# A second fp16 form of the exponential on VectorE, in a fused attention and feed-forward kernel

## The chip, the cores and the metric

One core of a Trainium2 chip runs the whole kernel. The metric is the device time of one execution in microseconds (us); lower is better. Engines are named as in the profile: PE (TensorE), DVE (VectorE), ACT (ScalarE), POOL (GpSimd), SP (SyncE, which issues the DMAs).

## What is computed

One transformer block in bf16 with S = 2048 tokens, width D = 512, 32 heads of 16, and a feed-forward part (FFN) of width 1792:

```python
def reference(A_x, A_wqkv, A_wo, B_x, B_w_gate, B_w_up, B_w_down):
    def _A_ref(x, wqkv, wo):
        ...
        scores = jnp.einsum("bhqd,bhkd->bhqk", q, k) * (Dh ** -0.5)
        p = _softmax(scores, axis=-1)
        o = jnp.einsum("bhqk,bhkd->bhqd", p, v)
        return (lambda x, *d: x.transpose(*d))(o, 0, 2, 1, 3).reshape(B, S, D) @ wo
    def _B_ref(x, w_gate, w_up, w_down):
        return (_gelu(x @ w_gate) * (x @ w_up)) @ w_down
    x = A_x
    h = x + _A_ref(_layernorm(x, axis=-1), A_wqkv, A_wo)
    h2 = h + _B_ref(_layernorm(h, axis=-1), B_w_gate, B_w_up, B_w_down)
    return h2
```

The softmax has 32 x 2048 x 2048 exponentials. They are most of the elementwise work.

## The kernel before

The program holds two complete versions of the block, one behind the other.

**`fast_path`** comes first. It does not subtract a row maximum. Queries are taken in chunks of 512, 512, 512, 256 and 256 rows (`CHUNKS`); a unit is one chunk times one group of four heads, so there are NU = 40 units, 24 of 512 rows and 16 of 256. The scores come transposed, in tiles of 128 keys x 512 columns, one PSUM bank each, 2048 tiles in all. `qk` multiplies the tiles, alternately three and two banks at a time (`SLOTS`), `exps` has ACT write exp of them to the bf16 ring `PT` (line 1221), and `pv` multiplies the result by `VA`, the values with a 17th column that sums the weights, into one accumulator bank. A share of the tiles goes to DVE instead: `dget` opens groups of up to four tiles, `dconv` (line 1527) converts a tile of scores to uint16 in `dX`, `dchain` (lines 1540 to 1547) makes two factors from the group by bit operations and multiplications, `dE2` and `dX`, and `pv` multiplies both by `VA` and adds them. Python code that runs before the launch lays out the order of all engines' instructions: a list of streams with priorities, estimated durations and gates (`Sched`). Groups are opened where that plan has DVE free: at most one in `DGAP` = 6 us, at most `NX` = 3 not yet consumed, and only when the chain of the group before has passed the point where `gw` counts up.

At a unit's end `ofin` copies the accumulator, transposes it and takes the reciprocal of the sums into `LINV`, a tile of 128 x 40 units x 16 columns (line 1621): 16 columns for a unit of 512 rows, `4 * nb` = 8 for one of 256. `consts` sets all of `LINV` to 1.0 at the start (line 1250). `masks` writes one column, `probe`, that shows how a float beyond uint16 is converted.

**The check and the guard.** Near the end `check` (from line 1782) compares: `LCHK` is `LINV` clipped from below and above, made 1.0 where the clipped value equals `LINV` and 0.0 where not, over all 640 columns, with the probe's comparison in column 641. The minimum of the row goes to `lmin`, a matmul sums the 128 partitions, and the sum is put in `flag`. Every engine ends its part of the fast path with this (line 1088 is the load of the flag):

```python
r = h.alloc_register("flag_" + name)
h.reg_load(r, flag[0:1, 0:1])
with h.If_ne(r, 128):
    for sem, v in fin:
        if v:
            h.wait_ge(sem, v)
    FP.run(name, h)
```

**`max_path`**, which `FP.run` issues, computes the same block from the inputs again, with the row maximum. Its units are 4 chunks x 8 head groups = 32 units of 64 tiles. A fixed order of ticks is written out: 32 ticks for a unit, and the second pass starts `P2_START` = 42 ticks behind the first. In a tick, PE multiplies two score tiles for the first pass (`p1_pair`, three banks in turn) and two for the second (`p2_pair`, three other banks in turn), as one group that has all waits in front; DVE takes the maximum of the first two (`p1_consume`, `tensor_reduce`, 128 x 512 from PSUM); ACT takes exp of the other two, one bank each (`p2_consume`). Every fourth tick eight products with the values follow (`pv_burst`), in the other ticks a piece of the dense work (projections, output product, FFN), whose results ACT evacuates. Per unit four small DMAs put the negated maximum into rows of `QT`. After the last tick the last chunk's output product and FFN run by themselves.

Of the kernel before, what the change touches and what calls it, by code (L numbers as in the profile page):

```python
# [163 lines left out]
BF16 = mybir.dt.bfloat16  # L164
# [889 lines left out]
GS = 4  # L1054
# [5 lines left out]
DGAP = 6.0  # L1060
DBUSY = 2.0
LN2 = 0.6931471805599453
CENTER = 40
EC, EB, EK = 0.45805388, 1.01669147, 0.16656247
VSCALE = 2.0 ** (127 - CENTER)


def bass_sequential_preLN__mha_block__geglu_ffn__prompt_kernel(nc, A_x, A_wqkv, A_wo, B_x, B_w_gate, B_w_up, B_w_down, out):
# [37 lines left out]
def fast_path(nc, P, base0, ARENA, pbank, flag, A_x, A_wqkv, A_wo, B_x, B_w_gate, B_w_up, B_w_down, out):  # L1106
# [3 lines left out]
    def at(name, shape, dt, off=None):  # L1110
        nb = DTS[dt]
        for d_ in shape[1:]:
            nb *= d_
        if off is None:
            off = cur[0]
            cur[0] = (off + nb + 31) // 32 * 32
        assert off + nb <= ARENA, ("SBUF arena overflow", name, off, nb, ARENA)
        return nc.alloc_sbuf_tensor_at(name, shape, dt, offset=base0 + off)
# [6 lines left out]
    offX = cur[0]  # L1125
    dX = at("dX", [128, NX, GS, 512], U16)
    dW = at("dW", [128, GS, 512], F16)
    dE2 = at("dE2", [128, NE, GS, 512], BF16)
    gset = at("gset", [128, 1], FP32)
    probe = at("probe", [128, 2], U16)  # L1130
    offE = cur[0]
# [88 lines left out]
    def ACTF(o, i, func, **kw):  # L1220
        return lambda e: e.activation(out=o, in_=i, func=func, **kw)  # L1221
# [23 lines left out]
    def consts():  # L1245
        yield Op("pool", 0.5, lambda e: e.memset(ones_bf[:], 1.0), writes=["ones_bf"])
        yield Op("pool", 0.3, lambda e: e.affine_select(out=ident[:], in_=ones_bf[:, 0:128], pattern=[[1, 128]], compare_op=ALU.is_equal, fill=0.0,
                                                        base=0, channel_multiplier=-1), reads=["ones_bf"], writes=["ident"])
        yield Op("pool", 0.1, lambda e: e.memset(nhalf[:], -0.5), writes=["nhalf"])
        yield Op("pool", 0.2, lambda e: e.memset(LINV[:], 1.0), writes=[("LINV", u) for u in range(NU)])  # L1250
        yield Op("pool", 0.1, lambda e: e.memset(zero_bf[:], 0.0), writes=["zero_bf"])
        yield Op("pool", 0.3, lambda e: e.tensor_copy(out=ident32[:], in_=ident[:]), reads=["ident"], writes=["ident32"])
        yield Op("pool", 2.3, lambda e: e.memset(VA[:, :, :, 16:17], VSCALE), writes=["VA_ones"])

    def masks():
        for par in range(2):
            iv = ident32[:].rearrange("p (g x i) -> p g x i", g=4, x=2)[:, :, par, :]
            yield Op("dve", 0.2, lambda e, iv=iv, par=par: e.tensor_reduce(out=qmask[:, par:par + 1], in_=iv, axis=AX.XY, op=ALU.add), reads=["ident32"], writes=[("qm", par)])
            yield Op("dve", 0.1, lambda e, par=par: e.tensor_scalar(out=qmask[:, par:par + 1], in0=qmask[:, par:par + 1], scalar1=256.0 / LN2, scalar2=None, op0=ALU.mult),
                     reads=[("qm", par)], writes=[("qm", par)])  # L1260
        yield Op("dve", 0.5, lambda e: e.memset(pbank[:, PVB, :], 0.0), writes=[("pb", PVB)])
        yield Op("dve", 0.1, lambda e: e.tensor_scalar(out=probe[:, 0:1], in0=ident32[:, 0:1], scalar1=1e6, scalar2=0.0, op0=ALU.add, op1=ALU.max), reads=["ident32"], writes=["probe"])


    def ln1(c):
# [97 lines left out]
    def proj_v():  # L1363
        for t in range(NT):
            rd = ["wB", ("xnT", t)]
            mev.prio = T0 + 2 + 1.8 * t
            b = yield Acquire(reads=rd)
            for hf in range(2):
                yield Op("pe", 2 * TMM, cols=1024, fns=[MM(pbank[:, b, :], xnT[:, dc, 128 * t:128 * t + 128], wqkv_sb[:, dc, 2 * D:3 * D], dc == 0, dc == 3)
                                      for dc in (2 * hf, 2 * hf + 1)], reads=rd, writes=[("pb", b)])  # L1370
            op = Op("dve", 0.61, lambda e, b=b, t=t: e.tensor_scalar(out=VA[:, t, :, 0:16], in0=pbank[:, b, :].rearrange("p (h i) -> p h i", i=16), scalar1=VSCALE, scalar2=None, op0=ALU.mult),
                    reads=[("pb", b)], writes=[("V", t)])
            sch.add(v_evac(op, b), mev.prio)

# [105 lines left out]
    def exps():  # L1480
        st = 0
        while "qkdone" not in C or st < len(STEPS):
            if st >= len(STEPS):
                yield Wait(lambda: st < len(STEPS))
            an, mine, b0 = STEPS[st]
            p0, n = an % NRING, len(mine)
            yield Op("act", 0.093 + 0.427 * n, ACTF(PT[:, p0:p0 + n, :], pbank[:, b0:b0 + n, :], ACT.Exp, scale=LN2 / 1024, bias=-LN2 * (127 - CENTER) - math.log(EC)),
                     reads=[("pb", b0 + k) for k in range(n)], writes=[("PT", p0 + k) for k in range(n)],
                     gate=lambda: C.get("qk", 0) >= st + 1 and C["acons"] >= an + n - NRING)
            st += 1  # L1490
            C["exp"] = st
            made.update(mine)
        C["expdone"] = 1
        sch.early = True
        for b0, n in SLOTS:
            for b in range(b0, b0 + n):
                sch.release(b)
# [26 lines left out]
                C["dbanks"].append(b)  # L1524

    def dconv(G, j, b):
        yield Op("dve", 0.7, lambda e: e.tensor_scalar(out=dX[:, G["k"] % NX, j, :], in0=pbank[:, b, :], scalar1=1024.0 * CENTER, scalar2=0.0, op0=ALU.add, op1=ALU.max),  # L1527
                 reads=[("pb", b)], writes=[("dX", G["k"] % NX, j)], gate=lambda: C["gpv"] >= G["k"] - NX + 1)
        sch.release(b)
        G["conv"] += 1  # L1530

    def dchain(G):

        d, x, n = G["k"] % NE, G["k"] % NX, len(G["t"])
        X, W, E = dX[:, x, 0:n, :], dW[:, 0:n, :], dE2[:, d, 0:n, :]
        M, T = X.bitcast(F16), X.bitcast(BF16)
        kX, kW, kE = [("dX", x, j) for j in range(n)], ["dW"], [("dE", d)]
        t1, t2 = 0.16 + 0.133 * n, 0.16 + 0.267 * n
        yield Wait(lambda: G["conv"] == n)
        yield Op("dve", t1, lambda e: e.tensor_scalar(out=E.bitcast(U16), in0=X, scalar1=3, scalar2=0x1f80, op0=ALU.logical_shift_right, op1=ALU.bitwise_and), reads=kX, writes=kE,  # L1540
                 gate=lambda: C["gpv"] >= G["k"] - NE + 1)
        yield Op("dve", t1, lambda e: e.tensor_scalar(out=X, in0=X, scalar1=0x3ff, scalar2=0x3c00, op0=ALU.bitwise_and, op1=ALU.bitwise_or), reads=kX, writes=kX)  # L1542
        yield Op("dve", t2, lambda e: e.tensor_tensor(out=W, in0=M, in1=M, op=ALU.mult), reads=kX, writes=kW)  # L1543
        yield Op("dve", t1, lambda e: e.tensor_scalar(out=W, in0=W, scalar1=EK, scalar2=EB, op0=ALU.mult, op1=ALU.add), reads=kW, writes=kW)
        yield Op("dve", t2, lambda e: e.tensor_tensor(out=W, in0=W, in1=M, op=ALU.mult), reads=kW + kX, writes=kW)  # L1545
        C["gw"] += 1
        yield Op("dve", t2, lambda e: e.tensor_tensor(out=T, in0=W, in1=E, op=ALU.mult), reads=kW + kE, writes=kX)  # L1547
        G["done"] = 1

    def pv():  # L1550
# [17 lines left out]
        for u in range(NU):  # L1568
# [4 lines left out]
            for m in range(nm):  # L1573
# [4 lines left out]
                for G in groups.get(u, ()):  # L1578
                    if "done" in G and "pv" not in G and m:
                        d, x = G["k"] % NE, G["k"] % NX  # L1580
                        fns = []
                        for j, i in enumerate(G["t"]):
                            fns += prod(i, [dE2[:, d, j, :], dX[:, x, j, :].bitcast(BF16)])
                        fns = [f for _, f in sorted(fns, key=lambda a: a[0])]
                        kts = sorted({TILES[i][1] * r + e for i in G["t"] for e in range(r)})
                        yield Op("pe", 2 * TPV + 0.1 * (r - 1), cols=256 * len(G["t"]), fns=fns, reads=[("V", kt) for kt in kts] + ["VA_ones", ("dE", d)] + [("dX", x, j) for j in range(len(G["t"]))], writes=[("pb", PVB)],
                                 gate=lambda: C["oa"] >= u)
                        G["pv"] = 1
                        C["gpv"] += 1
# [191 lines left out]
    def check():  # L1781
        yield Wait(lambda: C.get(("hnT", NC - 1), 0) == CHUNKS[-1] // 128)
        lf = LINV[:].rearrange("p u i -> p (u i)")
        n = NUNIT * 16
        yield Op("dve", 0.1, lambda e: e.tensor_scalar(out=LCHK[:, n:n + 1], in0=probe[:, 0:1], scalar1=65535.0, scalar2=None, op0=ALU.is_equal), reads=["probe"] + [("LINV", u) for u in range(NU)], writes=["probe", "LCHK"])
        yield Op("dve", 0.4, lambda e: e.tensor_scalar(out=LCHK[:, 0:n], in0=lf, scalar1=2.0 ** -22, scalar2=2.0 ** 16, op0=ALU.max, op1=ALU.min),
                 reads=[("LINV", u) for u in range(NU)], writes=["LCHK"])
        yield Op("dve", 0.6, lambda e: e.tensor_tensor(out=LCHK[:, 0:n], in0=LCHK[:, 0:n], in1=lf, op=ALU.is_equal), reads=["LCHK"], writes=["LCHK"])
        yield Op("dve", 0.6, lambda e: e.tensor_reduce(out=lmin[:, 0:1], in_=LCHK[:], axis=AX.X, op=ALU.min), reads=["LCHK", "probe"], writes=["lmin"])
# [93 lines left out]
```

## Time and profile before

| quantity | value |
|---|---|
| three runs | 949.26 us median (949.03 to 950.34) |
| the profiled execution | 948.94 us, of which the span from first to last instruction is 947.0 us |
| PE / DVE / ACT / POOL busy | 88% / 78% / 92% / 23% of the span |
| exps on ACT | 733 instructions, 841.0 us |
| conversions on DVE (`dconv`) | 216, 146.8 us |
| chains on DVE (`dchain`) | 64 groups |
| granted TensorE clock | 0.994 |

The profile is one execution on the core. A row of the costliest groups reads: line, engine, operation, output<-input with shapes, count, then busy time and the mean ns of one instruction, then the idle time of the engine just before and what ended it. The chain of waits is followed back from the last instruction, and gives the share of each engine on it. No instruction of `max_path` is in this trace: the 17699 instructions are those of the fast path.

### The profile page before, as it was taken

What the parts mean: (1) busy time and instruction counts of PE and PEld (TensorE: products, weight loads), DVE (VectorE), ACT (ScalarE), POOL (GpSimd) and SP (SyncE); (2) the same over time, 40 slices, a digit from 0 to 9 for tenths busy, and PEclk for the clock granted to TensorE, in tenths of its full rate; (3) what the DMA queues carried; (4) which work ended last, traced back from release to release, by engine and by line L of the source; (5) the groups of instructions that cost most, each with busy time, mean ns of one, the idle gap of its engine ahead of it and who ended that gap; (6) DMA issues with size and microseconds to landing.
All of it is one profiled execution on the core that took longest, in us unless ns stands there. A gap on an engine that the chain in (4) does not pass through costs nothing.

```text
span 947.0 us, 17699 instructions
## 1 busy us (share of the span) xinstructions
PE 833.2 (88%) x7100; PEld 276.3 (29%) x7224; DVE 735.3 (78%) x1138; ACT 874.4 (92%) x817; POOL 220.5 (23%) x268
## 2 busy tenths in 40 slices
PE   8999888888898889888888988998898788899887
PEld 3322222222232222222222222222233222333345
DVE  7558989998979768699979788889958687643753
ACT  5789999999999999999999998999999799999962
POOL 6400000000027570000014564000003354302440
PEclk9999999999999999999999999999999899999999
DMA  5000006000000000000000000000000000000000
GB/s 178 1 1 1 1 1 244 1 2 1 12 2 1 1 1 12 23 1 2 1 12 1 1 1 1 12 23 1 1 8 19 1 1 1 2 12 24 2 7 21
DMA packets 12331, 15.13 MB, mean 16 GB/s; under 512 B 1744, under 2 KB 11216, under 8 KB 12240
## 3 DMA queue, kind: packets, MB, share of 16 engines
q1 hardware_dynamic: 12240, 13.90, 4.5%
q8 instruction: 59, 0.97, 0.5%
q14 instruction: 32, 0.26, 0.1%
HBM read 11.80 MB, written 2.10 MB: 15 GB/s over the span
## 4 chain that ended last, share of the span: by engine, by line
ACT 33%; PE 32%; DVE 16%; issue 14%; POOL 5%; ACTq 0%; DVEq 0%; POOLq 0%
ACT PT L1221 32%; PE pbank L1215 15%; PE pbank L1214 11%; PE pbank L1801 4%; POOL w_sb L1717 2%; DVE dX L1527 2%; POOL w_sb L1719 2%; DVE dW L1543 2%; DVE dE_56 L1540 1%; DVE dX L1542 1%; DVE dX L1547 1%; DVE g_sb L1715 1%; ACT w_sb L1726 1%; POOL w_sb L1718 1%; DVE w_sb L1727 1%
## 5 line engine op out<-in xcount | busy, mean ns | idle before, releaser
L1221 ACT ACTIVATE PT<-pbank 128x1536 bf16<-128x1536 f32 (+1 forms) x733 | 841.0, 1306 | 24.8 <-PE pbank L1215 24.2
L1215 PE MATMUL pbank<-QT,KT 32*128 32x512 bf16 (+1 forms) x2560 | 287.1, 341 | 71.7 <-ACT PT L1221 57.5
L1215 PE MATMUL pbank<-PT,VA 128*17 128x512 bf16 (+1 forms) x2307 | 187.6, 340 | 3.2 <-issue 1.8
L1527 DVE TENSOR_SCALAR dX<-pbank 128x512 uint16<-128x512 f32 x216 | 146.8, 686 | 45.9 <-PE pbank L1215 45.0
L1215 PEld LDWEIGHTS pbank<-QT,KT 32*128 32x128 bf16 x2560 | 77.0, 91 | 319.3 <-ACT PT L1221 220.6
L1801 PE MATMUL pbank<-ones_bf,zero_bf 128*128 128x512 bf16 x388 | 135.2, 388 | 13.5 <-DVE OA L1613 11.0
L1678 POOL TENSOR_SCALAR rstd_102<-mv_101 128x1 f32<-128x1 f32 x16 | 4.3, 269 | 510.4 <-DVE mv_101 L1676 510.3
L1717 POOL TENSOR_TENSOR w_sb<-g_sb 128x512 f32<-128x512 f32 (+1 forms) x56 | 65.3, 1166 | 168.2 <-DVE g_sb L1715 168.2
L1215 PEld LDWEIGHTS pbank<-PT,VA 128*17 128x17 bf16 x2307 | 47.5, 87 | 110.6 <-issue 98.1
L1547 DVE TENSOR_TENSOR dX<-dW,dE_56 128x2048 bf16<-128x2048 f16 (+3 forms) x64 | 73.2, 1144 | 1.0
L1719 POOL TENSOR_TENSOR w_sb<-w_sb,g_sb 128x512 f32<-128x512 f32 (+1 forms) x56 | 71.3, 1273 | 4.7
L1545 DVE TENSOR_TENSOR dW<-dW,dX 128x2048 f16<-128x2048 f16 (+3 forms) x64 | 71.0, 1109 | 1.4
L1543 DVE TENSOR_TENSOR dW<-dX 128x2048 f16<-128x2048 f16 (+3 forms) x64 | 70.7, 1105 | 1.2
L1801 PEld LDWEIGHTS pbank<-ones_bf,zero_bf 128*128 128x128 bf16 x459 | 37.3, 97 | 78.3 <-issue 61.7
L1727 DVE SCALAR_TENSOR_TENSOR w_sb<-w_sb,g_sb 128x512 f32<-128x512 f32 (+1 forms) x56 | 44.1, 787 | 20.6 <-ACT w_sb L1726 20.2
L1214 PE MATMUL pbank<-wd_sb,GUT 128*128 128x512 bf16 x211 | 56.0, 381 | 1.5 <-issue 1.3
L1715 DVE COPY g_sb<-pbank 128x512 f32<-128x512 f32 (+1 forms) x56 | 34.7, 619 | 18.6 <-PE pbank L1214 18.5
L1753 DVE SCALAR_TENSOR_TENSOR GUT<-pbank,w_sb 128x512 bf16<-128x512 f32 (+1 forms) x56 | 34.6, 619 | 15.5 <-PE pbank L1214 15.2
L1726 ACT ACTIVATE w_sb<-w_sb 128x512 f32<-128x512 f32 (+1 forms) x56 | 34.1, 609 | 12.4 <-POOL w_sb L1719 12.4
L1718 POOL TENSOR_SCALAR w_sb<-w_sb 128x512 f32<-128x512 f32 (+1 forms) x56 | 43.6, 779 | 4.9
L1540 DVE TENSOR_SCALAR dE_56<-dX 128x2048 uint16<-128x2048 uint16 (+3 forms) x64 | 43.5, 680 | 0.6
L1542 DVE TENSOR_SCALAR dX<-dX 128x2048 uint16<-128x2048 uint16 (+3 forms) x64 | 42.9, 670 | 1.2
(126 smaller groups left out, 694.0 us busy)
## 6 DMA issues: line engine op xcount, KB each, us to landing
xres<-in_A_x_dram SPq DMA_DIRECT2D x16, 128.0 KB, 2.2
out_dram<-out_sb SPq DMA_DIRECT2D x16, 128.0 KB, 1.7
wg_sb<-in_B_w_gate_dram SPq DMA_DIRECT2D x1, 1792.0 KB, 7.1
wu_sb<-in_B_w_up_dram SPq DMA_DIRECT2D x1, 1792.0 KB, 11.2
wd_sb<-in_B_w_down_dram SPq DMA_DIRECT2D x1, 1792.0 KB, 17.0
x_sb<-in_A_x_dram SPq DMA_DIRECT2D x3, 512.0 KB, 8.3
wqkv_sb<-in_A_wqkv_dram SPq DMA_DIRECT2D x1, 896.0 KB, 7.5
x_sb<-in_A_x_dram SPq DMA_DIRECT2D x2, 256.0 KB, 2.9
```

Source lines behind the costliest of these rows:

```text
L1214: return lambda e: e.matmul(o, l, r, start=start, stop=stop)
L1215: return lambda e: e.matmul(o, l, r, start=start, stop=stop, tile_position=tile)
L1221: return lambda e: e.activation(out=o, in_=i, func=func, **kw)
L1527: yield Op("dve", 0.7, lambda e: e.tensor_scalar(out=dX[:, G["k"] % NX, j, :], in0=pbank[:, b, :], scalar1=1024.0 * CENTER, scalar2=0.0, o ...
L1543: yield Op("dve", t2, lambda e: e.tensor_tensor(out=W, in0=M, in1=M, op=ALU.mult), reads=kX, writes=kW)
L1545: yield Op("dve", t2, lambda e: e.tensor_tensor(out=W, in0=W, in1=M, op=ALU.mult), reads=kW + kX, writes=kW)
L1547: yield Op("dve", t2, lambda e: e.tensor_tensor(out=T, in0=W, in1=E, op=ALU.mult), reads=kW + kE, writes=kX)
L1717: yield Op("pool", 0.1 + 1.03 * nq / 512, lambda e: e.tensor_tensor(out=ws, in0=gs, in1=gs, op=ALU.mult), reads=[("g", i)], writes=[("w", i)])
L1718: yield Op("pool", 0.1 + 0.7 * nq / 512, lambda e: e.tensor_scalar(out=ws, in0=ws, scalar1=GA, scalar2=1.0, op0=ALU.mult, op1=ALU.add), re ...
L1719: yield Op("pool", 0.1 + 1.2 * nq / 512, lambda e: e.tensor_tensor(out=ws, in0=ws, in1=gs, op=ALU.mult), reads=[("w", i), ("g", i)], write ...
L1727: yield Op("dve", 0.1 + 0.7 * nq / 512, lambda e: e.scalar_tensor_tensor(out=ws, in0=ws, scalar=1.0, in1=gs, op0=ALU.add, op1=ALU.mult), r ...
L1801: fill_op = Op("pe", TMM, lambda e: e.matmul(pbank[:, PVB, :], zero_bf[:], ones_bf[:], start=False, stop=False, skip_group_check=True), re ...
```

## The change

DVE's part of the exponentials is written in fp16 with exponents from 0 to 29. The uint16 from `dconv`, read as fp16, is itself a factor of the second product, so the polynomial has one multiplication fewer; the first product has the power of two alone. The scale that was in `VA` (2 to the power 127 - `CENTER`) goes: the 17th column is 1.0, and the values are copied. The bias of ACT's exp follows. The conversion now clips at the top only. The bounds of `check` and its probe follow the new scale.

```diff
-CENTER = 40
-EC, EB, EK = 0.45805388, 1.01669147, 0.16656247
-VSCALE = 2.0 ** (127 - CENTER)
+XMAX = 30.0 * 1024 - 1
+CENTER = 12
+EC, EK = 0.46167356, 0.16665046
...
-    dE2 = at("dE2", [128, NE, GS, 512], BF16)
+    dE2 = at("dE2", [128, NE, GS, 512], F16)
...
-        yield Op("pool", 2.3, lambda e: e.memset(VA[:, :, :, 16:17], VSCALE), writes=["VA_ones"])
+        yield Op("pool", 2.3, lambda e: e.memset(VA[:, :, :, 16:17], 1.0), writes=["VA_ones"])
...
-        yield Op("dve", 0.1, lambda e: e.tensor_scalar(out=probe[:, 0:1], in0=ident32[:, 0:1], scalar1=1e6, scalar2=0.0, op0=ALU.add, op1=ALU.max), reads=["ident32"], writes=["probe"])
+        yield Op("dve", 0.1, lambda e: e.tensor_scalar(out=probe[:, 0:1], in0=ident32[:, 0:1], scalar1=-1e6, scalar2=XMAX, op0=ALU.add, op1=ALU.min), reads=["ident32"], writes=["probe"])
...
-            op = Op("dve", 0.61, lambda e, b=b, t=t: e.tensor_scalar(out=VA[:, t, :, 0:16], in0=pbank[:, b, :].rearrange("p (h i) -> p h i", i=16), scalar1=VSCALE, scalar2=None, op0=ALU.mult),
+            op = Op("dve", 0.61, lambda e, b=b, t=t: e.tensor_copy(out=VA[:, t, :, 0:16], in_=pbank[:, b, :].rearrange("p (h i) -> p h i", i=16)),
...
-            yield Op("act", 0.093 + 0.427 * n, ACTF(PT[:, p0:p0 + n, :], pbank[:, b0:b0 + n, :], ACT.Exp, scale=LN2 / 1024, bias=-LN2 * (127 - CENTER) - math.log(EC)),
+            yield Op("act", 0.093 + 0.427 * n, ACTF(PT[:, p0:p0 + n, :], pbank[:, b0:b0 + n, :], ACT.Exp, scale=LN2 / 1024, bias=-LN2 * (15 - CENTER) - math.log(EC)),
...
-        yield Op("dve", 0.7, lambda e: e.tensor_scalar(out=dX[:, G["k"] % NX, j, :], in0=pbank[:, b, :], scalar1=1024.0 * CENTER, scalar2=0.0, op0=ALU.add, op1=ALU.max),
+        yield Op("dve", 0.7, lambda e: e.tensor_scalar(out=dX[:, G["k"] % NX, j, :], in0=pbank[:, b, :], scalar1=1024.0 * CENTER, scalar2=XMAX, op0=ALU.add, op1=ALU.min),
...
-        M, T = X.bitcast(F16), X.bitcast(BF16)
+        L = X.bitcast(F16)
...
-        yield Op("dve", t1, lambda e: e.tensor_scalar(out=E.bitcast(U16), in0=X, scalar1=3, scalar2=0x1f80, op0=ALU.logical_shift_right, op1=ALU.bitwise_and), reads=kX, writes=kE,
+        yield Op("dve", t1, lambda e: e.tensor_scalar(out=W.bitcast(U16), in0=X, scalar1=0x3ff, scalar2=0x3c00, op0=ALU.bitwise_and, op1=ALU.bitwise_or), reads=kX, writes=kW)
+        yield Op("dve", t2, lambda e: e.tensor_tensor(out=W, in0=W, in1=W, op=ALU.mult), reads=kW, writes=kW)
+        yield Op("dve", t1, lambda e: e.tensor_scalar(out=W, in0=W, scalar1=EK, scalar2=1.0, op0=ALU.mult, op1=ALU.add), reads=kW, writes=kW)
+        yield Op("dve", t1, lambda e: e.tensor_scalar(out=E.bitcast(U16), in0=X, scalar1=0x7c00, scalar2=None, op0=ALU.bitwise_and), reads=kX, writes=kE,
                  gate=lambda: C["gpv"] >= G["k"] - NE + 1)
-        yield Op("dve", t1, lambda e: e.tensor_scalar(out=X, in0=X, scalar1=0x3ff, scalar2=0x3c00, op0=ALU.bitwise_and, op1=ALU.bitwise_or), reads=kX, writes=kX)
-        yield Op("dve", t2, lambda e: e.tensor_tensor(out=W, in0=M, in1=M, op=ALU.mult), reads=kX, writes=kW)
-        yield Op("dve", t1, lambda e: e.tensor_scalar(out=W, in0=W, scalar1=EK, scalar2=EB, op0=ALU.mult, op1=ALU.add), reads=kW, writes=kW)
-        yield Op("dve", t2, lambda e: e.tensor_tensor(out=W, in0=W, in1=M, op=ALU.mult), reads=kW + kX, writes=kW)
         C["gw"] += 1
-        yield Op("dve", t2, lambda e: e.tensor_tensor(out=T, in0=W, in1=E, op=ALU.mult), reads=kW + kE, writes=kX)
+        yield Op("dve", t2, lambda e: e.tensor_tensor(out=L, in0=W, in1=L, op=ALU.mult), reads=kW + kX, writes=kX)
...
-                            fns += prod(i, [dE2[:, d, j, :], dX[:, x, j, :].bitcast(BF16)])
+                            fns += prod(i, [dE2[:, d, j, :], dX[:, x, j, :].bitcast(F16)])
...
-        yield Op("dve", 0.1, lambda e: e.tensor_scalar(out=LCHK[:, n:n + 1], in0=probe[:, 0:1], scalar1=65535.0, scalar2=None, op0=ALU.is_equal), reads=["probe"] + [("LINV", u) for u in range(NU)], writes=["probe", "LCHK"])
-        yield Op("dve", 0.4, lambda e: e.tensor_scalar(out=LCHK[:, 0:n], in0=lf, scalar1=2.0 ** -22, scalar2=2.0 ** 16, op0=ALU.max, op1=ALU.min),
+        yield Op("dve", 0.1, lambda e: e.tensor_scalar(out=LCHK[:, n:n + 1], in0=probe[:, 0:1], scalar1=0.0, scalar2=None, op0=ALU.is_equal), reads=["probe"] + [("LINV", u) for u in range(NU)], writes=["probe", "LCHK"])
+        yield Op("dve", 0.4, lambda e: e.tensor_scalar(out=LCHK[:, 0:n], in0=lf, scalar1=2.0 ** -16, scalar2=2.0 ** -7, op0=ALU.max, op1=ALU.min),
                  reads=[("LINV", u) for u in range(NU)], writes=["LCHK"])
```

## The prediction

> **What bounds the kernel now.** I read the page's totals and chain of waits first, then the tiles of the check, since the diff moves the bounds of a comparison that decides whether a second kernel runs.
>
> ```profile
> span 947.0 us, 17699 instructions
> ...
> PE 833.2 (88%) x7100; PEld 276.3 (29%) x7224; DVE 735.3 (78%) x1138; ACT 874.4 (92%) x817; POOL 220.5 (23%) x268
> ...
> ACT 33%; PE 32%; DVE 16%; issue 14%; POOL 5%; ACTq 0%; DVEq 0%; POOLq 0%
> ...
> L1221 ACT ACTIVATE PT<-pbank 128x1536 bf16<-128x1536 f32 (+1 forms) x733 | 841.0, 1306 | 24.8 <-PE pbank L1215 24.2
> ...
> L1545 DVE TENSOR_TENSOR dW<-dW,dX 128x2048 f16<-128x2048 f16 (+3 forms) x64 | 71.0, 1109 | 1.4
> ```
>
> ACT's exps bound the fast path: 841.0 us in a span of 947.0. DVE has 22% idle and takes over 216 of 2048 tiles. L1545 is the multiplication that the change drops.
>
> The tile LINV, by the lines that write and read it:
>
> ```profile
> L1621 DVE RECIPROCAL LINV<-pbank x40: 190/247/258, 63.8 to 913.9; 128x16 f32<-128x16 f32 x24, 128x8 f32<-128x8 f32 x16
> ...
> L1250 POOL MEMSET LINV<- x1: 631/631/631, 1.7 to 1.7; 128x640 f32 x1
> L1786 DVE TENSOR_SCALAR LCHK<-LINV x1: 494/494/494, 922.7 to 922.7; 128x640 f32<-128x640 f32 x1
> L1788 DVE TENSOR_TENSOR LCHK<-LCHK,LINV x1: 824/824/824, 923.2 to 923.2; 128x640 f32<-128x640 f32 x1
> ```
>
> This is the view that decides. The memset writes 640 columns of 1.0. The reciprocals then write 24 x 16 + 16 x 8 = 512 of them. So 128 columns, the upper halves of the 16 units of 256 rows, still hold 1.0 when the check reads all 640.
>
> The tile flag, the tile LCHK, the groups kept apart by shape, and the timeline of DVE:
>
> ```profile
> L1792 DVE CAST flag<-pbank x1: 135/135/135, 935.9 to 935.9; 1x1 int32<-1x1 f32 x1
> L1088 ACTq TENSOR_LOAD <-flag x1: 468/468/468, 936.1 to 936.1; - x1
> ...
> L1088 SPq TENSOR_LOAD <-flag x1: 481/481/481, 943.0 to 943.0; - x1
> ```
>
> ```profile
> L1789 DVE TENSOR_REDUCE lmin<-LCHK x1: 823/823/823, 924.1 to 924.1; 128x1 bf16<-128x641 f32 x1
> ```
>
> ```profile
> L1221 ACT ACTIVATE PT<-pbank 128x1536 bf16<-128x1536 f32 x366 | 555.3, 1517 | 21.1 <-PE pbank L1215 20.5
> L1221 ACT ACTIVATE PT<-pbank 128x1024 bf16<-128x1024 f32 x367 | 402.1, 1096 | 3.7 <-PE pbank L1215 3.7
> ```
>
> ```profile
> 444.16 1.28 DVE L1527 TENSOR_SCALAR dX<-pbank 128x512 uint16<-128x512 f32 x2
> ```
>
> All engines read the flag between 936 and 943 us and leave. These durations are my prices for the second kernel.
>
> **What the Trainium skill says.** "VectorE: DVE Perf Modes", section "The perf-mode tier table", has 16-bit tensor_tensor at two and tensor_scalar at four elements a cycle, 1224 and 693 ns for 2048 elements, and tensor_reduce at one. The trace agrees: 1248 ns (L1545) and 708 ns (L1544) at 128x2048, and 823 ns for the reduce of 641. "Perfetto Trace Analysis", section "Optimizing Scalar/DVE Operations", says that half of an instruction's fixed latency overlaps with the next one; the pair above agrees: two conversions of 686 ns end after 1.28 us, so the second starts 0.59 us after the first. "Runtime: NRT & Kernel Launch", section "Instruction fetch mechanics", says that a branch out of the fetched window stalls for a fetch; nothing before prices that.
>
> **The change, part by part.**
>
> *The check.* With the new upper bound, 1.0 is clipped to 2^-7 = 0.0078, which does not equal 1.0. Those 128 columns become 0 in every partition, the minimum is 0, the sum is 0, not 128, and every engine enters the guarded block: it waits for all fast-path work and runs max_path. The old bound, 2^16, let 1.0 pass. No line of the diff writes the 128 columns or narrows what is read. If the new probe did not come out as 0 (the trace shows no conversion below zero), the result would be the same.
>
> *The fast path.* It drops 64 multiplications, 71.0 us of DVE (L1545); the other two keep their 16-bit type and price. A DVE tile costs now (146.8 conversions + 43.5 + 42.9 + 70.7 + 71.0 + 73.2 on the page + 40.6 for L1544: 29.7 + 5.7 + 3.7 and about 1.5 for the smallest) / 216 = 2.26 us, afterwards (488.7 - 71.0) / 216 = 1.93. If all freed time went to more tiles, it would carry 71 / 1.93 = 37, each worth 841.0 / 1832 = 0.46 us on ACT: 17 us. If none did, nothing: the plan also asks for free banks, 6 us between groups and unconsumed groups below three. I take half, 8 us, so a span of 939. Nearby edits cost nothing: the copy of VA stays a 690 ns evacuation, the mask that moves to fourth place only reads X, and gw counts a little earlier. fp16 tiles against bf16 values have no row; if those 506 products took twice as long, PE would pay up to the 54.7 us of their rows (19.6 + 19.5 + 7.8 + 7.8); I take 0, since both are 16-bit.
>
> *max_path, added behind it.* Counted from the code, it has 1066 ticks (42 + 32 x 32). Per tick DVE does two maxima of 128x512 from PSUM. One takes 512/641 of the reduce's 668 ns streaming (641 at one per cycle, estimated by the skill's rate at 0.96 GHz) plus the remaining 155: 688 ns, like a conversion (686). Back to back, two take 2 x 0.594 = 1.19 if they overlap like conversions, 1.38 if not at all. ACT does two exps of one bank: 1517 - 1096 = 421 ns a bank, 841.0/733 - 2.5 x 421 = 94 ns fixed, so 515 ns queued, 1.03 a tick. PE needs 0.39 for the score group and 0.45 to 0.8 for the rest. So DVE sets the tick; I take 1.24, near the overlapping end, with 0.05 for the round trip maximum, wait, next score group (0.44 from a score group's start at 445.93 to its consumer at 446.37). 1066 x 1.24 = 1322 us.
>
> *ACT's evacuations in it.* 353 ticks, again counted, have one more ACT instruction (74 projections, 94 for unit ends, 185 for the first three chunks' output and FFN). Such a tick needs 3 x 0.515 = 1.55 on ACT against 1.24. The next score group waits for exp through a ring of three banks, which absorbs little, so 0.31, and a bit for evacuations behind late matmuls: 0.35 x 353 = 124 us. The ends: 0 if neighbouring ticks absorb it, 0.48 (687 ns unqueued, L1356, less 0.21 slack).
>
> *The rest of it.* Start after the branch 4 us (0 to 8, unpriced). Before the first tick: 16 x (0.67 + 0.18) statistics, 12 x 0.40 normalisations, about 2 for the padded copy, loads of 3 and five projections of some 1.5: 32 with waits (25 to 40). Unit ends: 32 small maxima of 0.25 = 8. 256 bursts of products that hold PE a little too long, 0.04 each: 10. After the last tick: last unit 4, four output tiles at 2 us of POOL each plus 3, 28 x 4 x 0.22 = 25 for gate and up, 5 x 15 x 0.22 = 16 for down, last transfer 3: 59 us. All of this lies on the path, as nothing else runs.
>
> Sum: 939 + 4 + 32 + 1322 + 124 + 8 + 10 + 59 = 2498 us of span. Around it the profiled execution has 948.94 - 947.0 = 1.9, which gives 2500 us. That execution is 0.3 below the median of the runs, which at this size says nothing.
>
> **The rivals.** *B: the second kernel runs, and ACT's evacuations are hidden.* For it: DVE pairs at 1.19 as measured, ACT only 85% full. Against it: three banks per pass and one wait for both. 939 + 4 + 30 + 1066 x 1.19 + 18 + 57 = 2317 us. *C: the second kernel runs, and its maxima don't overlap, or the small DMAs with the maxima come late.* For it: the row is 686 without overlap; a unit's maxima have ten ticks, 12 us, for a POOL chain, transposes, an evacuation and a DMA of 2 to 3 us. 939 + 4 + 32 + 1066 x 1.38 + 353 x 0.17 + 18 + 59 = 2583, up to 2650 with 2 us lost per unit. *D, on the other side: the check passes, and only the fast path runs,* 939 + 2 = 941 us, faster. Its place is line 1786, its price nothing, and it decides from the point where all 640 columns lie within 2^-16 and 2^-7. For it: only that the diff means the bounds to fit the new sums. Against it: the 128x8 reciprocals above leave 1.0 behind.
>
> **How the numbers follow.** Forecast 0.58, B 0.14, C 0.22, D 0.06. The time is the forecast's, 2500. The range 2330 to 2680 holds the forecast with its bounds and most of B and C; it leaves out D and their far ends. By over 0.2% (what a measurement of this kernel can tell from no change): slower 0.94; D splits into faster 0.05 and within 0.2% 0.01.
>
> **What would show it.** The changed profile must show the load of the flag followed by thousands of instructions with lines below 800 in a span over two times as long: 2046 maxima at line 506 and 2048 exps at line 557. Their start shows the fast path's length (930 to 950), the distance of exps per tick shows 1.24 and what an evacuation adds, and the DVE rows before the branch show 64 or more chains with one multiplication fewer. A trace without those lines makes the forecast wrong at its root; ticks at 1.4 or at 1.2 throughout make it wrong in size.

## The result, and the profile after

The changed kernel takes 2408.2 us (median of four runs, 2407.57 to 2409.85) against 949.14 us (median of four, 945.87 to 950.34). The ratio is 2.539, with a 95% interval from 2.532 to 2.545. The profiled execution took 2407.61 us, with a span of 2405.7.

The page of the changed kernel, with the lines that answer to those of before:

```profile
span 2405.7 us, 42193 instructions
...
PE 1928.5 (80%) x15458; PEld 580.1 (24%) x15722; DVE 1993.0 (83%) x3273; ACT 2157.4 (90%) x3284; POOL 669.6 (28%) x857
...
ACT 35%; DVE 23%; PE 22%; issue 17%; POOL 2%; DMA 1%; SPq 0%; ACTq 0%; POOLq 0%; DVEq 0%
...
L506 DVE TENSOR_REDUCE mx_PM<-pbank 128x1 f32<-128x512 f32 x2048 | 1257.4, 683 | 68.8 <-PE pbank L547 57.8
L557 ACT ACTIVATE mx_PT<-pbank 128x512 bf16<-128x512 f32 x2048 | 1117.2, 602 | 79.7 <-PE pbank L547 9.1
L1221 ACT ACTIVATE PT<-pbank 128x1536 bf16<-128x1536 f32 x727 | 833.7, 1301 | 18.3 <-PE pbank L1215 17.7
...
L1547 DVE TENSOR_TENSOR dX<-dW,dX 128x2048 f16<-128x2048 f16 (+3 forms) x69 | 77.4, 1122 | 1.2
```

There are 24494 more instructions, and the costliest two lines, 506 and 557, belong to max_path. The exps of the fast path are still there beside them, with 69 chains in place of 64. So both kernels ran. The share of busy time on ACT (90%) looks as it did before (92%), which tells nothing of the doubled work: the span of the page and the line numbers of its groups do.

The tiles LINV and flag of the changed kernel, by the lines that write and read them:

```profile
L1621 DVE RECIPROCAL LINV<-pbank x40: 195/251/259, 64.0 to 891.9; 128x16 f32<-128x16 f32 x24, 128x8 f32<-128x8 f32 x16
...
L1250 POOL MEMSET LINV<- x1: 632/632/632, 1.7 to 1.7; 128x640 f32 x1
```

```profile
L1088 SPq TENSOR_LOAD <-flag x1: 487/487/487, 927.8 to 927.8; - x1
```

Nothing has changed in who writes LINV: 640 columns by the memset, 512 by the reciprocals. The flag is read by SP at 927.8 us; before, it was read at 943.0. The fast path is 15 us shorter in this execution. What follows it, in the timeline of the changed kernel (start and duration in us, engine, line):

```profile
927.41 0.33 SPq L1774 DMA_DIRECT2D out_dram<-out_sb  x1
929.20 2.04 SPq L273 DMA_DIRECT2D mx_x_sb<-in_A_x_dram  x4
929.25 0.53 POOL L278 MEMSET mx_ones_bf<- 128x512 bf16 x1 [29.14 <-DMA out_dram<-out_sb]
...
961.48 0.39 PE L497 MATMUL pbank<-mx_KT,mx_QT 32*128 32x512 bf16 x2 [0.69 <-ACT mx_QT L419]
```

The last output of the fast path is issued, lands, and 1.8 us after its issue max_path begins from the inputs; its first score group starts 32 us later. The span in the stages of the forecast, from the table by stretches (us, then each engine's busy time and count of instructions, granted clock, share and rate of the DMAs):

```profile
929.20:961.50 32.30, 12.91 (x85) 8.32 (x86) 18.09 (x48) 11.93 (x21) 22.29 (x29) 0.58 0.37 131
961.50:1019.80 58.30, 53.95 (x247) 16.73 (x252) 53.67 (x85) 26.05 (x41) 1.01 (x4) 0.97 0.00 1
1019.80:2336.00 1316.20, 979.65 (x7787) 255.52 (x7917) 1209.78 (x1996) 1236.50 (x2387) 424.28 (x534) 1.00 0.02 8
2336.00:2405.70 69.70, 54.97 (x241) 24.58 (x245) 19.43 (x31) 15.87 (x26) 11.52 (x22) 0.82 0.06 18
```

| stage | forecast (us) | measured (us) |
|---|---|---|
| fast path and the start after the branch | 939 + 4 = 943 | 929.2 |
| before the first tick | 32 | 32.3 |
| the 1066 ticks | 1322 + 124 + 8 + 10 = 1464 | 58.3 + 1316.2 = 1374.5 |
| after the last tick | 59 | 69.7 |
| span | 2498 | 2405.7 |

The measured span lies halfway between the forecast's 2498 and rival B's 2317.

### The profile page after: what moved, and what is told of

Read it like the earlier page. It is cut to its first block, busy times and chain, and to the rows that moved or that the text cites. A ratio compares the mean times of both kernels' runs of the same rounds, so it can differ in the third digit from the quotient of the medians.

```text
span 2405.7 us, 42193 instructions
## 1 busy us (share of the span) xinstructions
PE 1928.5 (80%) x15458; PEld 580.1 (24%) x15722; DVE 1993.0 (83%) x3273; ACT 2157.4 (90%) x3284; POOL 669.6 (28%) x857
## 4 chain that ended last, share of the span: by engine, by line
ACT 35%; DVE 23%; PE 22%; issue 17%; POOL 2%; DMA 1%; SPq 0%; ACTq 0%; POOLq 0%; DVEq 0%
DVE mx_PM L506 19%; ACT mx_PT L557 16%; ACT PT L1221 15%; PE pbank L497 7%; PE pbank L1215 6%; PE pbank L1214 4%; PE pbank L1801 1%; PE pbank L547 1%; PE pbank L772 1%; PE pbank L729 1%; ACT mx_OA L419 1%; PE pbank L748 1%; ACT mx_u_sb L419 0%; DVE g_sb L1715 0%; POOL w_sb L1719 0%
## 5 line engine op out<-in xcount | busy, mean ns | idle before, releaser
L506 DVE TENSOR_REDUCE mx_PM<-pbank 128x1 f32<-128x512 f32 x2048 | 1257.4, 683 | 68.8 <-PE pbank L547 57.8
L557 ACT ACTIVATE mx_PT<-pbank 128x512 bf16<-128x512 f32 x2048 | 1117.2, 602 | 79.7 <-PE pbank L547 9.1
L1221 ACT ACTIVATE PT<-pbank 128x1536 bf16<-128x1536 f32 x727 | 833.7, 1301 | 18.3 <-PE pbank L1215 17.7
L497 PE MATMUL pbank<-mx_KT,mx_QT 32*128 32x512 bf16 x2048 | 398.8, 383 | 316.7 <-DVE mx_PM L506 165.7
L547 PE MATMUL pbank<-mx_QT,mx_KT 32*128 32x512 bf16 x2048 | 397.8, 385 | 4.9 <-ACT mx_PT L557 4.4
L497 PEld LDWEIGHTS pbank<-mx_KT,mx_QT 32*128 32x128 bf16 x2048 | 105.0, 91 | 781.7 <-DVE mx_PM L506 772.7
L788 PE MATMUL pbank<-mx_ones_bf,mx_ident 128*128 128x512 bf16 x756 | 239.2, 385 | 5.0 <-ACT mx_PT L557 3.5
L591 POOL TENSOR_TENSOR mx_LINV<-mx_OAT,mx_negone 128x16 f32<-128x16 f32 x32 | 93.3, 2916 | 331.0 <-ACT mx_OAT L419 331.0
L568 PE MATMUL pbank<-mx_PT,mx_VA 128*17 128x512 bf16 x2048 | 156.8, 383 | 0.0
L547 PEld LDWEIGHTS pbank<-mx_QT,mx_KT 32*128 32x128 bf16 x2048 | 96.1, 91 | 23.6 <-ACT mx_PT L557 23.0
```

The costliest lines, as they stand in the source:

```text
L497: P.op("pe", lambda e, g=g, b=b: e.matmul(pbank[:, b, :], QT[32 * g:32 * g + 32, c, slot, 128 * qt:128 * qt + 128], KT[32 * g:32 * g + 32, ...
L506: P.op("dve", lambda e, b=b, qt=qt, kc=kc, g=g: e.tensor_reduce(out=PM[:, par, qt, kc, g:g + 1], in_=pbank[:, b, :], axis=AX.X, op=ALU.max ...
L547: P.op("pe", lambda e, g=g, b=b: e.matmul(pbank[:, b, :], KT[32 * g:32 * g + 32, slot, 128 * kt:128 * kt + 128], QT[32 * g:32 * g + 32, c, ...
L557: P.op("act", lambda e, b=b, pi=pi: e.activation(out=PT[:, pi, :], in_=pbank[:, b, :], func=ACT.Exp), reads=[("pb", b)], writes=[("PT", pi)])
L568: P.op("pe", lambda e, g=g, kt=kt, pi=pi, slot=slot: e.matmul(pbank[32 * g:32 * g + 17, PVB, :], VA[:, kt, 4 * slot + g, :], PT[:, pi, :], ...
L591: P.op("pool", lambda e: e.tensor_tensor(out=li, in0=oat4[:, :, :, 16], in1=negone[:].rearrange("p (q g) -> p q g", g=4), op=ALU.pow), rea ...
```

## The experiments

The kernel before took 948.02 us (median of 11) beside e1, e2, e4 and e5, 949.94 (once) beside e6 and e7, and 948.27 (median of 15) beside e8 to e11. Where only a part of a line changes, the edit shows that part. "Fill" in a name means that the start value of LINV was made to lie inside the new bounds.

**Is it the 128 columns?** One number of the changed kernel is edited (e1_fill):

```diff
-memset(LINV[:], 1.0)
+memset(LINV[:], 2.0 ** -9)
```

> The changed kernel, with the start value of LINV set to 2 to the power -9 in place of 1.0, so that the 128 columns that no unit writes lie inside the new bounds. Theory (only these columns fail): the sum is 128, max_path is not entered, no line below 800 is in the trace, and the time is that of the fast path alone, which ends 15 us earlier than before: about 934 us. Rival (the probe does not come out as 0, or true sums lie outside the bounds): still some 2408 us.

It took 934.73 us (six runs, 933.83 to 939.48), a ratio of 0.986 [0.984, 0.987] to the kernel before. Its profiled execution was the slowest of the six, with this page:

```profile
span 937.6 us, 17691 instructions
...
ACT 40%; PE 32%; issue 17%; DVE 8%; POOL 3%; ACTq 0%; DVEq 0%; POOLq 0%
```

No instruction of max_path is left. The new probe, the new sums and all the fp16 arithmetic are in this kernel, and yet the second kernel isn't entered, so none of them is the reason: the stale 1.0 is.

**Is the bound alone enough?** The kernel before, with only its upper bound edited (e2_bound):

```diff
-scalar1=2.0 ** -22, scalar2=2.0 ** 16
+scalar1=2.0 ** -22, scalar2=2.0 ** -7
```

> The kernel before, with one edit: the upper bound of the check is 2 to the power -7 in place of 2 to the power 16. Theory (the bound alone enters the second kernel): the fast path as before, then max_path, 947 - 2 + 1476 + 2 = about 2423 us. Rival (the fp16 sums or the probe do it): 949 us.

It took 2424.06 us (one run). Its page, and its timeline behind the flag:

```profile
span 2422.1 us, 42201 instructions
```

```profile
945.45 2.04 SPq L273 DMA_DIRECT2D mx_x_sb<-in_A_x_dram  x4
```

The old arithmetic with the new bound runs max_path too, from 945.45 us on, and 2422.1 - 945.45 = 1476.7 us long, the same as the 2405.7 - 929.2 = 1476.5 of the changed kernel. So the whole loss comes from this one number, where it meets columns that still hold 1.0.

**What does the second kernel cost by itself?** max_path alone (e6_maxalone):

```diff
-        fast_path(nc, P, base0, ARENA, pbank, flag, *args)
...
         def emit(name, h):
-            P.run(name, h)
...
-                FP.run(name, h)
...
+            FP.run(name, h)
```

> max_path alone: the fast path, the check and the guard are left out. Theory (the second kernel is simply added behind the first, with little lost at the branch): its first DMA in the changed kernel starts at 929.2 of 2405.7 us, so 1476.5 us of span, about 1478 us. Rival (the branch or a cold start costs ten us or more within these 1476): below 1468 us.

It took 1474.6 us, with a span of 1472.9: 3.6 us less than behind the fast path, by one execution of each. So to start behind the branch costs at most a few us more than to start alone. The Trainium skill, in "Runtime: NRT & Kernel Launch", section "Instruction fetch mechanics", says that a taken branch out of the fetched window stalls for a fetch; no run here shows such a stall by itself, and one that a start alone has too would not show in this difference. Its ticks repeat those of the changed kernel: a tick whose predecessor had no evacuation on ACT takes 1.19 us (median of 674, start of one second-pass score group to the next, in ticks with both passes), one whose predecessor had an evacuation 1.46 (308).

**What sets the tick?** First the maxima over half of their columns (e7_halfmax):

```diff
-in_=pbank[:, b, :], axis=AX.X, op=ALU.max
+in_=pbank[:, b, 0:256], axis=AX.X, op=ALU.max
```

> max_path alone, with each maximum of the first pass over 256 of its 512 columns (half of the maximum is left out). Theory (a plain tick is set by two maxima at 0.594 us, and ACT's exps with an evacuation stand close behind): plain ticks go from 1.19 to about 1.08, as in the last 42 ticks of the changed kernel, where no maxima run, a tick with an evacuation adds 0.5 in place of 0.28, and the whole goes from 1478 to about 1430 us. Rival (the maxima alone are the bound throughout): ticks of 0.66, and a whole below 1150 us.

Both expectations missed. It took 1471.85 us, 2.75 less than e6_maxalone (one execution of each), although DVE's busy time fell from 1300.9 to 820.2 us. Groups of e7_halfmax, then its ticks:

```profile
L557 ACT ACTIVATE mx_PT<-pbank 128x512 bf16<-128x512 f32 x2048 | 1117.9, 603 | 74.4 <-PE pbank L547 8.0
L506 DVE TENSOR_REDUCE mx_PM<-pbank 128x1 f32<-128x256 f32 x2048 | 774.3, 420 | 542.7 <-PE pbank L547 508.1
```

```profile
771.45 0.39 PE L497 MATMUL pbank<-mx_KT,mx_QT 32*128 32x512 bf16 x2 [0.25 <-ACT mx_PT L557]
...
771.89 0.76 DVE L506 TENSOR_REDUCE mx_PM<-pbank 128x1 f32<-128x256 f32 x2 [0.43 <-PE pbank L547]
...
772.63 0.39 PE L497 MATMUL pbank<-mx_KT,mx_QT 32*128 32x512 bf16 x2
```

DVE now idles 542.7 us before line 506, and the tick is 1.18 all the same. The score group waits for ACT: 899 times in the whole trace (283.5 us), where in e6_maxalone it waited 621 times for DVE (157.2 us) and 298 times for ACT (140.5). With two of three banks written in each tick, the next score group needs the bank of the first exp of the tick before. In the medians of plain ticks it takes 0.43 us from the start of a score group to the start of that exp, 0.60 for the exp, and 0.15 from its end to the next score group: 1.18. Between its pairs of exps ACT still idles 0.10 us, so it isn't short of time; the chain of these three steps is a second constraint, a round trip through the ring of three banks, of the same length as two maxima (2 x 0.594 = 1.19). Two more runs were made to tell this from a delay by the order of the maxima. Half of each exp (e8_halfexp), with a start value in the ring:

```diff
-out=PT[:, pi, :], in_=pbank[:, b, :], func=ACT.Exp
+out=PT[:, pi, 0:256], in_=pbank[:, b, 0:256], func=ACT.Exp
```

> max_path alone, with each exp of the second pass over 256 of its 512 columns (half of the exponentials is left out; the ring starts at 1.0). Halving the maxima alone moved nothing, since the round trip score group, exp, next score group takes the same 1.18 us as two maxima. Theory (two constraints of the same length, and ACT's evacuations add about 0.28 us each, through that round trip): plain ticks stay at 1.19 by the maxima, and the evacuations are hidden, as ACT has 0.4 us more room: 1473 - 353 x 0.28 = about 1375 us. Rival (the maxima's two-by-two order alone delays the ticks with evacuations): about 1470 us.

It took 1393.54 us, and both kinds of ticks take 1.20: the evacuations are hidden, as the theory has it. After the exp, which takes 0.38 us now, 0.37 us pass to the next score group in place of 0.15: the round trip has room, and the maxima set the tick. The timeline of e8_halfexp shows an evacuation, with the ticks on both sides of it:

```profile
701.19 0.60 ACT L420 ACTIVATE mx_out_sb<-pbank 128x512 bf16<-128x512 f32 x1
701.20 0.39 PE L498 MATMUL pbank<-mx_KT,mx_QT 32*128 32x512 bf16 x2
...
702.39 0.39 PE L498 MATMUL pbank<-mx_KT,mx_QT 32*128 32x512 bf16 x2 [0.27 <-DVE mx_PM L507]
...
703.59 0.39 PE L498 MATMUL pbank<-mx_KT,mx_QT 32*128 32x512 bf16 x2
```

Then both halves (e9_bothhalf, the two edits together):

> max_path alone, with both the maxima and the exps over 256 of 512 columns (half of each is left out). Theory (two constraints of the same length): only now do plain ticks shorten, to the round trip with a shorter exp, 1.18 - 0.2 = 0.98 us, or to PE's own work of about 1.0, so 1375 - 1066 x 0.2 = about 1170 us. Rival (a third engine holds the tick at 1.18): about 1375 us.

It took 1203.46 us; ticks are 0.97 us without an evacuation in front and 1.04 with one. Only when both are shortened does the plain tick shorten. Its new length fits both of the expected bounds: a round trip with the shorter exp, 0.43 + 0.38 + 0.15 = 0.97, and PE's own work. The waits speak for PE: its score groups wait for ACT only 29 times in this run (5.7 us), and PE is busy for 90% of the span, against 77% in e7_halfmax. The totals of e8 and e9 lie 18 and 33 us above their estimates; what the rest is made of was not followed.

**What did the fast path gain?** These runs have 4 to 10 executions each. A sixth operation in the chain, whose output is overwritten (e4_sixth):

```diff
+        yield Op("dve", t2, lambda e: e.tensor_tensor(out=E, in0=W, in1=W, op=ALU.mult), reads=kW, writes=kE,
+                 gate=lambda: C["gpv"] >= G["k"] - NE + 1)
         yield Op("dve", t2, lambda e: e.tensor_tensor(out=W, in0=W, in1=W, op=ALU.mult), reads=kW, writes=kW)
```

> The kernel e1_fill with a sixth operation put back into the chain, a multiplication of the length of the dropped one, whose output is overwritten. The plan then gives DVE 214 tiles (before 216, change 231). Theory (what the fast path gains is the dropped multiplication, by way of more tiles on DVE and less DVE time): about 949 us, as before. Rival (the gain is in the fp16 form itself, its copies, masks or products): about 934 us.

The five operations, planned as if they took as long as the six (e5_oldplan):

```diff
-        yield Op("dve", t2, lambda e: e.tensor_tensor(out=W, in0=W, in1=W, op=ALU.mult), reads=kW, writes=kW)
+        yield Op("dve", 2 * t2, lambda e: e.tensor_tensor(out=W, in0=W, in1=W, op=ALU.mult), reads=kW, writes=kW)
```

> The kernel e1_fill, with the dropped multiplication's duration left in the plan: the chain has five operations, but the plan reckons with the old length, and gives DVE 206 tiles. Theory 1 (the gain is tiles that move from ACT to DVE): ACT has 25 tiles more than in e1_fill at 0.46 us, so 934 + 11 = 945 us or more. Theory 2 (the gain is that chains end earlier and what waits for them, with tiles of no account): about 934 us or less.

The kernel before with fewer tiles on DVE (e10_before_gap7), and e1_fill in another order (e11_fill_gap7), both by

```diff
-DGAP = 6.0
+DGAP = 7.0
```

> The kernel before, with its six operations, and 7 us in place of 6 between groups, which makes the plan give DVE 209 tiles in 62 groups (before 216 in 64). Theory 2 of the fast path (DVE with fewer hours of work is late less often, and tiles are of little account): 946 us or less. Theory 1 (tiles on ACT set the time): 948 + 7 x 0.46 = 951 us. A change of the plan alone may also move the time by some us either way.

> The kernel e1_fill with 7 us in place of 6 between groups: 231 tiles as in e1_fill, in 68 groups in place of 69, in another order. If the order of the plan is of no account: 934 us, as e1_fill. A difference shows how much the order alone moves, and so how far single microseconds between the plans can be read.

| kernel | operations | tiles on DVE | us | ratio to before |
|---|---|---|---|---|
| e1_fill | 5 | 231 | 934.73 | 0.986 [0.984, 0.987] |
| e11_fill_gap7 | 5 | 231 | 929.47 | 0.980 [0.978, 0.982] |
| e5_oldplan | 5 | 206 | 935.76 | 0.988 [0.986, 0.989] |
| e4_sixth | 6 | 214 | 956.34 | 1.010 [1.008, 1.012] |
| e10_before_gap7 | 6 (old form) | 209 | 952.87 | 1.005 [1.003, 1.007] |

The three kernels with five operations are faster than before, the two with six are not. Two of the expectations were missed: e4_sixth was to come back to 949 us and is 7 us above that, and e10_before_gap7 was to take 946 us or less by theory 2; its median is nearer to the 951 of theory 1.

The medians of e4_sixth and e10_before_gap7 can't be read as they stand, since their executions were granted lower clocks. TensorE's mean granted clock was 0.983 to 0.992 in those of e10_before_gap7 and 0.990 to 0.998 in those of the kernel before beside it, and in every kernel of the table the executions at a lower clock took longer on the whole (e10_before_gap7: 955.32 us at 0.983, 948.26 at 0.992). At 0.992, e10_before_gap7 took 948.26 us and the kernel before 949.95 to 950.19, so there, by one execution, it is 2 us faster, which fits neither theory. At 0.991 e4_sixth took 955.37 and 955.42 us, which stays some 5 us above the kernel before. Why these two plans ran at a lower clock was not followed.

Tiles alone don't set the time: e5_oldplan has 25 fewer on DVE than e1_fill and is 1.0 us slower, where 11 were expected from their price on ACT. With nearly the same tiles, 206 against 209, e5_oldplan is 17 us faster than e10_before_gap7 by the medians, and about 11 by the executions with the nearest clocks (937.37 at 0.994, 948.26 at 0.992). The chains of waits of the two:

```profile
ACT 46%; PE 28%; issue 18%; DVE 5%; POOL 1%; DMA 1%; SPq 0%; ACTq 0%; DVEq 0%
```

```profile
ACT 37%; PE 31%; issue 16%; DVE 12%; POOL 3%; DMA 1%; SPq 0%; ACTq 0%; DVEq 0%
```

Before, DVE held 16% of that chain, in e1_fill 8%, here 5% against 12%. ACT, which bounds this part, waits less: its time that is not busy is 947.0 - 874.4 = 72.6 us before and 933.4 - 876.8 = 56.6 in e5_oldplan. The waits of ACT (total, times, longest), before and in e5_oldplan, show where nearly all of these 16 us lie:

```profile
ACT PT L1221 <- PE pbank L1215: 24.2, 35, 2.8
ACT w_sb L1726 <- POOL w_sb L1719: 12.4, 15, 1.8
```

```profile
ACT PT L1221 <- PE pbank L1215: 19.2, 25, 2.8
ACT w_sb L1726 <- POOL w_sb L1719: 1.7, 5, 0.9
```

ACT got back 5.0 us in front of its exps and 10.7 us in front of the tanh of the FFN's gelu. That tanh waits for three operations on POOL (lines 1717 to 1719), and these for a copy on DVE (line 1715, `g_sb`), which stands in DVE's queue with the chains. The traces show both links a little shorter: the copy starts 0.37 us after the last gate product that ended before it (mean of 56), where it was 0.45 before and 0.53 in e10_before_gap7, and the three POOL operations on 512 columns take 3.6 us from start to end, where they took 3.8 in both. No run changed one of these alone, so how a shorter chain on DVE brings this about is argued, not shown. In e1_fill the gain looks different: ACT's busy time fell by 7.1 us (874.4 to 867.3), the price of the 15 tiles, and its idle time by only 2.3, in the slowest of its executions.

One more rival is open in part. In the old form the first operation of the chain writes `dE2` and needs a free buffer of it, in e4_sixth the second does, in the five-operation form the fourth. At run time DVE hardly waits there (0.6 us in all before line 1540 in the kernel before, 1.3 before line 1542 in e4_sixth), but what the place does to the order of the plan was not separated from the multiplication. The order of the plan alone moves some 5 us (e11_fill_gap7 against e1_fill, where no difference was expected if order is of no account), so none of these differences is to be read to the microsecond. The fp16 form itself brought no gain in e4_sixth, which keeps it and the old number of operations.

The quickest, e11_fill_gap7 at 929.47 us, is faster than both kernels of this case.

## Why the prediction was right

**The check.** Shown: with the bound alone the old kernel enters the second one, and with the 128 columns inside the bounds the changed kernel does not. The rival that lets the check pass (D) fell for the reason given, the reciprocals 128 x 8. It was to be read before the change was run, from the shapes of one tile's writers.

**The size.** That the second kernel runs was right by its reason; the size was less sure than the hit looks. The span came out 92 us below the forecast: 14 of them in the fast path and the start, 89 in the ticks, and 11 the other way after them. The result lies as near to rival B's sum, 2317, which is below the range's lower edge of 2330, although the prediction says that the range holds most of B.

**The fast path.** 13.3 us fewer in e1_fill (948.02 - 934.73) and 15.2 in the changed kernel (the last evacuation, line 1771, starts at 926.69 us and started at 941.85), where 8 was taken between 0 and 17. The sign was right, the way at best half: the gain was worked out as tiles that leave ACT, of which there were 15, worth 7 us, and ACT's busy time fell by that much; but e5_oldplan has the gain without such tiles, in shorter waits on ACT. What the prediction left out is that ACT's waits, too, can shorten with the chain on DVE; by which link they do is argued, not shown. The fast path ended just below the 930 to 950 us that were to be seen. That fp16 tiles against bf16 values cost PE nothing was right; the products of the changed kernel, apart by shape, take 384 and 379 ns where 388 and 385 stood:

```profile
L1215 PE MATMUL pbank<-dE_56,VA 128*17 128x512 f16 x192 | 20.6, 384 | 2.4 <-DVE dX L1547 1.3 <-DVE OA L1613 0.9
L1215 PE MATMUL pbank<-dX,VA 128*17 128x512 f16 x192 | 20.4, 379 | 0.0
```

The kept multiplications hold their price at 128x2048: 1263 ns (line 1542) and 1299 (line 1547) against 1242 and 1303 before. The Trainium skill's page "VectorE: DVE Perf Modes", section "The perf-mode tier table", has 1224 for a 16-bit tensor_tensor of this size; the trace is 3 to 6% above it.

**The ticks** were forecast too long by 1464 - 1374.5 = 89 us, the term that was mis-sized most. Two ticks of the changed kernel and the evacuation between them, in its timeline:

```profile
1701.38 0.39 PE L497 MATMUL pbank<-mx_KT,mx_QT 32*128 32x512 bf16 x2 [0.47 <-DVE mx_PM L506]
...
1701.60 0.60 ACT L419 ACTIVATE mx_OnT<-pbank 128x512 bf16<-128x512 bf16 x1
...
1702.08 3.48 ACT L557 ACTIVATE mx_PT<-pbank 128x512 bf16<-128x512 f32 x6
...
1702.84 0.39 PE L497 MATMUL pbank<-mx_KT,mx_QT 32*128 32x512 bf16 x2 [0.53 <-ACT mx_PT L557]
...
1704.04 0.39 PE L497 MATMUL pbank<-mx_KT,mx_QT 32*128 32x512 bf16 x2 [0.26 <-DVE mx_PM L506]
```

From 1701.38 to 1702.84 the tick takes 1.46: the evacuation stands before the exps on ACT, and the next score group waits for the first of them. From 1702.84 to 1704.04 it takes 1.20, and waits for DVE. A maximum does overlap with the next like a conversion, so a plain tick is 1.19, not 1.24: 1066 x 0.05 = 53 us. An evacuation adds 1.46 - 1.19 = 0.27, not 0.35: 353 x 0.08 = 28. The other 8 of the 89 us are spread over the allowances for unit ends and bursts and over the ends of the stage: the first 42 ticks took 1.39 each, with 58.3 us, and the last 42, without maxima, took mostly 1.08. The step "so DVE sets the tick" was half of the truth: e7_halfmax shows that ACT's round trip would set the same tick without DVE. The maxima are 2048, as counted from 32 units of 64 tiles; the 2046 of the prediction was a slip.

**Before and after the ticks.** 32.3 us against 32. After the last tick 69.7 against 59. Two things there are not named in the sum: one power on POOL for the last unit takes 2.9 us (line 591, mean 2916 ns), and TensorE's granted clock is 0.82 (last row of the table by stretches). How the 10.7 us divide was not worked out.

**The rivals.** B had hidden evacuations and the tick at 1.19: the tick is right, but the 308 ticks of 1.46 in max_path alone, and 299 waits of score groups for exps in the changed kernel, speak against the hiding, and e8_halfexp shows what it would take. C had maxima that don't overlap or late small DMAs: neither; waits of score groups for those DMAs are one of 6.5 us in the changed kernel.

## What to carry to other kernels

A new bound in a runtime check is part of the change: list who wrote each column that the check reads, with counts and shapes, and ask if the values that nobody wrote still pass. A guarded second kernel costs its whole length, and here its price could be estimated within 6% from durations of the first (1559 forecast with the start, 1476.5 measured). Where halving the work of the engine that seems to be the bound changes nothing, look for a round trip through a ring of buffers of the same length, and halve both. Before medians of two kernels are compared to a few us, look at the granted clocks of their executions.

## What the runs showed that was not expected

Two constraints of a tick agree within 0.01 us: two maxima at 1.19 and the round trip through three banks at 1.18. Taking more than a third off DVE's busy time (1300.9 to 820.2 us) won 2.75 us of 1474.6; shortening both won 271. And in the fast path a multiplication taken off an engine that was busy 78% of the time, and not the bound, went with 13 us of 948 by e1_fill, about 11 by e5_oldplan against e10_before_gap7 and 18 by e4_sixth against e1_fill (957.25 and 939.48, both at a granted clock of 0.988), more than the 7 us of the tiles that moved. In e5_oldplan, two thirds of the waiting that ACT got back (10.7 of 16.0 us) stood in front of the FFN's tanh and not in front of the exps.
